# Attention kernel's first 25 microseconds: first weights moved to ScalarE's queue behind its statistics, block 0 of x loaded in four pieces on two queues, first half of K turned ahead of the norms

## The chip, the cores and the metric

The kernel runs on one core of a Trainium2 chip. The metric is the device time of one execution in microseconds (us), median and mean over several runs, always compared with runs of the kernel before from the same rounds on the same chip. A profile is one traced execution of the same program; its span leaves out about 1.8 us that the device time includes (1939.6 against 1941.37 us in the profiled run of the kernel before).

Engine names: PE is TensorE (matmuls and transposes), PEld its weight loads, DVE is VectorE, ACT is ScalarE, POOL is GpSimd, SP is SyncE. A "q" (ACTq, SPq) marks an engine's sequencer issuing a DMA.

## The reference, cut to what matters

```python
def reference(A_x, A_k_cache, A_v_cache, A_wq, A_wo, B_x, B_w1, B_w3, B_w2):
    xn = layernorm(A_x)                     # 2048 x 640
    q  = (xn @ A_wq) in 32 heads of 192
    o  = softmax(q @ k_cache^T * 192**-0.5) @ v_cache     # per head, 2048 keys
    s  = o @ A_wo
    g  = silu((silu(xn @ B_w1) * (xn @ B_w3)) @ B_w2)     # hidden size 1536
    return A_x + s * g
```

The attention of 32 heads is nearly all of the work. Before its first score can be computed, the first block of x (512 rows) must be loaded, normalised, turned (transposed) and projected with the weights of head 0, and the first half of K must be loaded and turned.

## The kernel before: what the change touches

`load_x(g, t0, t1, queue)` loads tiles t0 to t1 of x's block g. `ln_stats`, `ln_rstd` and `ln_norm` are the norm on VectorE, with the reciprocal root on GpSimd; `ln_stats_act` does tile 3's statistics on ScalarE. `ln_turn` transposes two tiles on TensorE and copies the result to `xnT`; `kn` is K as loaded, `pk0` and `pk1` hold its turned halves in PSUM, `KW` holds them in SBUF; `swap_halves` makes a copy of xnT with its halves of the partitions exchanged, by DMA (`xnS`).

```python
    def load_w0():
        W = wqp.tile([P, 2 * DC, P], BF16, tag="W", name="W")
        nc.gpsimd.dma_start(out=W[:, 0:DC, :], in_=A_wq[:, 0:P]...)       # runs of 256 bytes
        nc.gpsimd.dma_start(out=W[:, DC:2 * DC, 0:PGW], in_=gate_cols(0)...)  # runs of 128 bytes
        nc.gpsimd.dma_start(out=W[:, DC:2 * DC, PGW:P], in_=A_wq[:, P:DH]...)
        ...
    def copy_k0(copy, src, half, two):          # a copy of turned K out of PSUM
        KW = loads[0]["KW"]
        ks = slice(half * HP * P, (half + 1) * HP * P)
        copy(out=KW[:, 0:2, ks] if two == 0 else KW[:, 2:5:2, ks], in_=src[:, 2 * two:2 * two + 2, :])
    ...
    pk1 = ps_o.tile([P, 4, 512], BF16, tag="ob1", name="pk1")    # two banks of PSUM
    warm = pk1[:, 0, 0:2 * P].bitcast(F32)

    def turn_over(k):                           # k dummy matmuls
        for i in range(k):
            nc.tensor.matmul(warm, lhsT=ident_bf[:], rhs=ident_bf[:], start=True, stop=True)

    def head_start():
        load_x(0, 0, 2)
        load_x(0, 2, 4)
        load_k0(0, nc.sync)                     # K of head 0, first half
        load_w0()
        turn_over(34)
        ln_stats(0, 0)
        ln_stats(0, 1)
        ln_stats_act(0, 3)
        load_k0(1, nc.scalar)
        load_x(1, queue=nc.scalar)
        load_v(0, (0,), nc.scalar)
        ln_stats(0, 2)
        ...                                     # two small VectorE instructions
        ln_rstd(0, 3)
        load_w(1)
        for i in range(4):
            ln_norm(0, i, nc.vector)
        pk0 = ps_o.tile([P, 4, 512], BF16, tag="ob0", name="pk0")
        turn_k0(pk0, 0, range(4))               # 16 transposes of K
        copy_k0(nc.scalar.copy, pk0, 0, 0)
        turn_over(4)
        ln_turn(0, 0, nc.scalar.copy)
        turn_k0(pk1, 1, (0, 1))                 # 8 transposes of K's second half
        ln_turn(0, 1, nc.vector.tensor_copy)
        swap_halves(0)
        copy_k0(nc.scalar.copy, pk0, 0, 1)
        copy_k0(nc.vector.tensor_copy, pk1, 1, 0)
        load_v(0, (1,))
        load_x(2)
        project_first()                         # the first projection
        turn_k0(pk1, 1, (2, 3))                 # the other 8
        copy_k0(nc.scalar.copy, pk1, 1, 1)
        scores(0)
        shift_first()                           # VectorE: two shifts of q
        shift_k0()                              # VectorE: "K shift", KW<-KW
        scores(1)
        ln_stats(1, 0)                          # the norms of block 1 follow
        ...
```

## Time and profile before

| | before |
|---|---|
| device time, first three runs | 1940.66, 1940.94, 1941.77 us |
| span of the profile | 1939.6 us |
| PE busy | 99% |
| PE share of the chain that ended last | 98% |
| PE time lost between matmuls after 62 us, as recorded | 1.3 us |

"Lost" in the last row is the sum of all stretches over 40 ns by which a matmul starts later than the columns of the matmul before it need at full clock. It is counted from the starts in the TensorE timeline. Most of it is not real: this profile has eight matmul records fewer than weight loads (see the counts below), and four of the eight stretches, of 0.22 to 0.23 us, are about as long as one matmul of 512 columns at full clock.

The first section and the chain section of the page of the kernel before (engine, busy us, share of the span):

```profile
PE 1928.9 (99%) x27267; PEld 1317.8 (68%) x27275; DVE 654.2 (34%) x997; ACT 1181.2 (61%) x1278; POOL 282.6 (15%) x501
...
PE 98%; DVE 1%; DMA 0%; ACT 0%; issue 0%; SPq 0%; POOL 0%; DVEq 0%; ACTq 0%
```

So the whole question is at what time TensorE gets into its steady rhythm. The TensorE timeline of the kernel before (start in us, duration, engine, line, operation, tiles, shape, count, and in brackets the idle time before and what ended it):

```profile
2.77 3.81 PE L569 MATMUL pk<-ident_bf 128*128 128x128 bf16 x34 [2.77 <-POOL ident_bf masks.py:199]
7.90 1.07 PE L271 MATMUL pk<-ident_bf,kn 128*128 128x128 bf16 x16 [1.32 <-DMA kn<-in_A_k_cache_dram]
...
9.03 0.72 PE L354 MATMUL pst<-ident_bf,xn 128*128 128x128 bf16 x10
...
11.20 2.34 PE L391 MATMUL ps<-xnT,W 128*128 128x256 bf16 x20 [0.44 <-ACT xnT L356]
```

and, from the timeline of its weight loads, the load that opens the turn of block 1's last tiles (the turn itself starts at 23.86):

```profile
23.85 0.56 PEld L354 LDWEIGHTS <-xn 128*128 128x128 bf16 x10 [0.36 <-DVE qA L429]
```

34 dummy matmuls keep TensorE busy while x and K arrive; TensorE pauses 1.32 us for K; x is turned at 9.03; the projection starts at 11.20. At 23.86 TensorE waits for VectorE's cast of qA. The VectorE timeline shows why:

```profile
11.53 0.68 DVE L277 COPY KW<-pk 128x1024 bf16<-128x1024 bf16 x1
...
13.58 0.42 DVE L393 CAST qA<-ps 128x256 bf16<-128x256 f32 x1 [0.67 <-PE ps L391]
...
14.88 0.42 DVE L281 COPY KW<-KW 64x1024 bf16<-64x1024 bf16 x1
15.33 0.89 DVE L316 BATCH_NORM_STATS2 stats<-x_all 128x6 f32<-128x320 bf16 x2
...
22.12 0.88 DVE L316 BATCH_NORM_STATS2 stats<-x_all 128x6 f32<-128x320 bf16 x2
23.04 0.21 DVE L317 BATCH_NORM_AGGREGATE mv<-stats 128x2 f32<-128x12 f32 x1
23.16 0.64 DVE L429 CAST qA<-ps 128x512 bf16<-128x512 f32 x1
```

From the first projection's casts on, VectorE works through copies, shifts and the norms of block 1 and the first of block 2 almost without a gap (one of 0.81 us, for GpSimd's reciprocal root), and the cast that TensorE needs stands in order behind all of it. From 15 to 24 us VectorE sets the pace. K's copy on VectorE at 11.53 falls into a lull before the casts.

### The profile page before, as it was taken

To read this page: it belongs to the slowest core of one execution; us is meant where nothing else is said; L and a number is where in the kernel's file an instruction comes from. 1 tells how busy PE (TensorE), PEld (TensorE's weight loads), DVE (VectorE), ACT (ScalarE), POOL (GpSimd) and SP (SyncE) were. 2 spreads that over 40 slices of the span, in tenths; PEclk is the share of its full clock that TensorE was granted. 3 is DMA by queue.
4 is the path that set the end of the run, shared out by engine and by line. 5 is a ranking of instruction groups with operands and counts; after the bars stand their busy time and mean duration, and the time that the engine had idled before them with its cause. 6 is when DMAs were issued, how large, how long until landed. Compare 5 with 4: busy or idle time off the path is not lost.

```text
span 1939.6 us, 59659 instructions
## 1 busy us (share of the span) xinstructions
PE 1928.9 (99%) x27267; PEld 1317.8 (68%) x27275; DVE 654.2 (34%) x997; ACT 1181.2 (61%) x1278; POOL 282.6 (15%) x501
## 2 busy tenths in 40 slices
PE   8999999999999999999999999999999999999998
PEld 6666666666666666666666666666666666577776
DVE  7333333333333333333333333333333334521111
ACT  6667676767776767776777777677767677210000
POOL 3111111111111111111111111111111110000000
PEclk9999999999999999999999999999999999999999
DMA  8643433323233434363434343434333220937882
GB/s 178 132 101 64 101 68 83 86 56 91 58 89 65 98 63 99 68 162 68 101 64 101 68 101 68 100 66 100 69 68 90 63 70 2 259 70 135 152 152 61
DMA packets 394643, 178.98 MB, mean 92 GB/s; under 512 B 341616, under 2 KB 382832, under 8 KB 394384
## 3 DMA queue, kind: packets, MB, share of 16 engines
q1 hardware_dynamic: 371136, 125.32, 30.9%
q0 software_dynamic: 19472, 45.71, 9.8%
q8 instruction: 215, 3.52, 0.8%
q10 hardware_dynamic: 3776, 4.06, 0.7%
q14 instruction: 44, 0.36, 0.1%
HBM read 52.82 MB, written 27.79 MB: 42 GB/s over the span
## 4 chain that ended last, share of the span: by engine, by line
PE 98%; DVE 1%; DMA 0%; ACT 0%; issue 0%; SPq 0%; POOL 0%; DVEq 0%; ACTq 0%
PE obank L516 35%; PE st L487 33%; PE ps L424 14%; PE ps_s L111 11%; PE ps_f L728 3%; PE ps_gu L702 1%; PE st L488 1%; PE ps L410 0%; DMA kn<-in_A_k_cache_dram 0%; DVE stats L316 0%; PE ps L391 0%; DVE xn L346 0%; DVE mv L317 0%; DVE qA L429 0%; ACT xnT L356 0%
## 5 line engine op out<-in xcount | busy, mean ns | idle before, releaser
L490 ACT ACTIVATE pT<-st 128x1024 bf16<-128x1024 f32 x1024 | 1047.1, 1023 | 251.1 <-PE st L488 235.6
L516 PEld LDWEIGHTS <-pT 64*128 64x128 bf16 x16384 | 713.7, 94 | 242.2 <-ACT pT L490 0.2
L516 PE MATMUL obank<-vt,pT 64*128 64x193 bf16 x16384 | 851.8, 243 | 0.0
L487 PE MATMUL st<-qC,KW 64*128 64x512 bf16 x2046 | 605.6, 376 | 0.1
L525 DVE COPY osum<-obank 128x772 f32<-128x772 f32 x128 | 123.1, 962 | 788.8 <-PE obank L516 788.8
L488 PE MATMUL st<-qB,KW 64*128 64x512 bf16 x1024 | 385.0, 376 | 0.0
L487 PE MATMUL st<-qA,KW 64*128 64x512 bf16 x1022 | 384.3, 376 | 0.4 <-ACT pT L490 0.3
L488 PE MATMUL st<-qC,KW 64*128 64x512 bf16 x1022 | 384.3, 376 | 0.0
L488 PE MATMUL st<-qA,KW 64*128 64x512 bf16 x1022 | 384.3, 376 | 0.0
L487 PEld LDWEIGHTS <-KW 64*128 64x128 bf16 x3068 | 278.0, 94 | 153.8 <-issue 2.1
L424 PE MATMUL ps<-xnT,W 64*128 64x512 bf16 x1280 | 297.2, 376 | 0.0
L424 PE MATMUL ps<-xnS,W 64*128 64x512 bf16 x1280 | 296.3, 376 | 0.0
L488 PEld LDWEIGHTS <-KW 64*128 64x128 bf16 x3068 | 278.0, 94 | 0.7 <-issue 0.6
L377 POOL DMA_DIRECT2D qC<-qA x124 | 65.4, 528 | 1285.6 <-DVE rl_all L532 1270.0
L430 ACT CAST qB<-ps 128x512 bf16<-128x512 f32 x131 | 76.8, 586 | 228.3 <-PE ps L424 222.7
L111 PE MATMUL ps_s<-wo_sb,oT 128*128 128x384 bf16 (+3 forms) x1535 | 208.8, 299 | 0.1
L424 PEld LDWEIGHTS <-W 64*128 64x128 bf16 x2560 | 122.9, 94 | 121.2
L111 PEld LDWEIGHTS <-oT 128*128 128x128 bf16 x1536 | 148.4, 98 | 60.4
L526 DVE TENSOR_TENSOR osum<-osum,obank 128x772 f32<-128x772 f32 x128 | 122.7, 958 | 13.4
L533 DVE TENSOR_TENSOR ostage<-osum,rl_all 128x768 bf16<-128x768 f32 x128 | 122.7, 958 | 4.4
L465 DVE SCALAR_TENSOR_TENSOR hT<-pt,qB 64x512 bf16<-64x512 bf16 x64 | 43.8, 684 | 199.4 <-ACT pt L464 199.4
L429 DVE CAST qA<-ps 128x512 bf16<-128x512 f32 x131 | 90.5, 691 | 25.2 <-PE ps L410 7.2
(84 smaller groups left out, 622.4 us busy)
## 6 DMA issues: line engine op xcount, KB each, us to landing
o_scr<-ostage SPq DMA_DIRECT2D x16, 1536.0 KB, 10.3
vt<-in_A_v_cache_dram SPq DMA_DIRECT2D x63, 384.0 KB, 5.7
qC<-qA POOLq DMA_DIRECT2D x248, 64.0 KB, 1.9
qC<-qB POOLq DMA_DIRECT2D x124, 64.0 KB, 2.4
wo_sb<-in_A_wo_dram POOLq DMA_DIRECT2D x1, 7680.0 KB, 36.2
W<-in_A_wq_dram POOLq DMA_DIRECT2D x32, 160.0 KB, 3.4
W<-in_B_w_dram POOLq DMA_DIRECT2D x32, 80.0 KB, 3.2
W<-in_A_wq_dram POOLq DMA_DIRECT2D x32, 80.0 KB, 2.9
```

Source lines behind the costliest of these rows:

```text
L111: nc.tensor.matmul(ps[:, 0:w], lhsT=oT[:, k, :], rhs=wo_sb[:, k, c0:c1], start=(k == 0), stop=(k == OC - 1))
L377: nc.gpsimd.dma_start(out=qC[0:64, half, :], in_=qAB[half][64:P, :])
L424: nc.tensor.matmul(ps[:, r * 512:(r + 1) * 512], lhsT=W[rows, j, :], rhs=xs[rows, j // 2, qs], start=(j == 0), stop=(j == 2 * DC - 1))
L429: a = nc.vector.tensor_copy(out=qAB[0][:], in_=ps[:, 0:512])
L430: b = nc.scalar.copy(out=qAB[1][:], in_=ps[:, 512:1024])
L487: nc.tensor.matmul(st2[:, 0:512], lhsT=ka, rhs=qa, start=r == 0 and nr == 3, stop=r == nr - 1)
L488: nc.tensor.matmul(st2[:, 512:1024], lhsT=kb, rhs=qb2, start=r == 0 and nr == 3, stop=r == nr - 1)
L490: nc.scalar.activation(out=pT2[:], in_=st2[:], func=ACT.Exp, scale=att_scale)
L516: nc.tensor.matmul(obanks[r][:, j * 256:j * 256 + DH + 1], lhsT=pT2[r * 64:(r + 1) * 64, t * 512 + j * P:t * 512 + (j + 1) * P], rhs=vt[r ...
L525: nc.vector.tensor_copy(out=osum[:], in_=ov[0])
L526: nc.vector.tensor_tensor(out=osum[:], in0=osum[:], in1=ov[1], op=ALU.add)
L533: nc.vector.tensor_tensor(out=ostage[:, qb * 4:qb * 4 + 4, hg * DH:(hg + 1) * DH], in0=osum[:, :, 0:DH], in1=rl.unsqueeze(2).to_broadcast( ...
```

## The change

Intent: get x and K in first, so that the first projection starts sooner, by keeping head 0's weights out of the first microseconds; and let ScalarE copy the turned x before it copies K. The diff, cut to its core:

```diff
-    def load_w0():
+    def load_w0(queue):
...     (nc.gpsimd.dma_start becomes queue.dma_start, three times)
@@ loads_after, in the middle of the kernel
-            for c0, c1 in _pieces(FC, -(-FC // 6)):
+            for c0, c1 in _pieces(FC, -(-FC // 2)):
@@ head_start
-        load_x(0, 0, 2)
-        load_x(0, 2, 4)
+        for t in range(4):
+            load_x(0, t, t + 1, nc.scalar if t % 2 else nc.sync)
         load_k0(0, nc.sync)
-        load_w0()
-        turn_over(34)
+        turn_over(24)
         ln_stats(0, 0)
         ln_stats(0, 1)
         ln_stats_act(0, 3)
+        load_w0(nc.scalar)
         load_k0(1, nc.scalar)
         load_x(1, queue=nc.scalar)
-        load_v(0, (0,), nc.scalar)
...
+        load_v(0, (0,), nc.gpsimd)
         load_w(1)
...
         turn_k0(pk0, 0, range(4))
-        copy_k0(nc.scalar.copy, pk0, 0, 0)
+        turn_over(12)
+        ln_turn(0, 0, nc.scalar.copy)
         turn_over(4)
-        ln_turn(0, 0, nc.scalar.copy)
-        turn_k0(pk1, 1, (0, 1))
         ln_turn(0, 1, nc.vector.tensor_copy)
         swap_halves(0)
+        copy_k0(nc.scalar.copy, pk0, 0, 0)
         copy_k0(nc.scalar.copy, pk0, 0, 1)
-        copy_k0(nc.vector.tensor_copy, pk1, 1, 0)
         load_v(0, (1,))
         load_x(2)
         project_first()
-        turn_k0(pk1, 1, (2, 3))
-        copy_k0(nc.scalar.copy, pk1, 1, 1)
+        turn_k0(pk1, 1, range(4))
+        copy_k0(nc.scalar.copy, pk1, 1, 0)
+        copy_k0(nc.vector.tensor_copy, pk1, 1, 1)
         scores(0)
```

The change also loads w2, used near the end, in two pieces instead of six.

More of the change, by code (lines that the diff above doesn't have):

```diff
@@ L219, in gate_cols @@
         return wsel[:, (h // 2) * PGW:(h // 2 + 1) * PGW]
-    def load_w0():
+    def load_w0(queue):
         W = wqp.tile([P, 2 * DC, P], BF16, tag="W", name="W")
-        nc.gpsimd.dma_start(out=W[:, 0:DC, :], in_=A_wq[:, 0:P].rearrange("(c p) d -> p c d", p=P))
-        nc.gpsimd.dma_start(out=W[:, DC:2 * DC, 0:PGW], in_=gate_cols(0).rearrange("(c p) f -> p c f", p=P))
-        nc.gpsimd.dma_start(out=W[:, DC:2 * DC, PGW:P], in_=A_wq[:, P:DH].rearrange("(c p) d -> p c d", p=P))
+        queue.dma_start(out=W[:, 0:DC, :], in_=A_wq[:, 0:P].rearrange("(c p) d -> p c d", p=P))
+        queue.dma_start(out=W[:, DC:2 * DC, 0:PGW], in_=gate_cols(0).rearrange("(c p) f -> p c f", p=P))
+        queue.dma_start(out=W[:, DC:2 * DC, PGW:P], in_=A_wq[:, P:DH].rearrange("(c p) d -> p c d", p=P))
         loads.setdefault(0, {}).update(W=W)
```

## The prediction

> **What bounds the kernel now.** The page puts PE busy at 99% of 1939.6 us and the chain that ended last at 98% PE. From the PE timeline, stretches where matmuls start further apart than their columns need add up to under 0.7 us after 60 us. Only the first 36 us can give anything back: 0.1% or so.
>
> **The start, before** (timelines by engine). x lands at 3.59 and 4.35 us; VectorE's statistics start at 3.62, norms 0 and 1 end at 7.93. K's first half, behind x, lands at 7.85, so PE idles 1.3 us (waits), turns K from 7.90, and first turns x at 9.03. ScalarE copies K (9.00) before xnT (9.91 to 11.14); the projection starts at 11.20. Its VectorE casts end at 14.00, three 0.29 us shifts and a 0.42 us K shift at 15.30; first exp at 15.05. VectorE then works almost unbroken to 23.80, where its cast of qA holds PE (0.29 us).
>
> **What the change does.**
> - Four x loads on two queues: the same bytes. The gain is the smaller first load, an estimated 0.4 us for VectorE's start; the Trainium skill, "DMA: Bandwidth & Descriptors", section "Issuing engines are not separate DMA queues", says more issuers save only issue time.
> - W of head 0 leaves the first microseconds: the identity may be ready at 1.7 instead of 2.7 us (GpSimd spends 1.02 us on a W load inside it), K's first half lands near 5.2. W, issued near 5.0-6.5 on ScalarE, should land by 9 (now 8.28).
> - K is turned before the norms end, so x's first turn follows norm 1 (7.6) and ScalarE copies xnT first: projection near 9.6, 1.6 us earlier.
> - But the second K half moves behind the projection: 16 transposes there instead of 8, and VectorE's 0.68 us copy, formerly in a lull at 11.53, now stands before the shifts. First exp near 13.7; K shift ends near 14.7, only 0.6 earlier.
> - Dummies 24+12+4 against 34+4 fill waits. The skill, "TensorE: Matmul & The Clock Gate", Part 1, says about 3.4 us of activity releases the clock; this trace agrees (107 ns steps until about 6.3 us, 56 later). The pause before K could delay that by some tenths.
> - w2 in two loads: issued at 844 us, first used at 1673. Nothing.
>
> **How much is critical.** PE and ScalarE get some 1.4 us ahead at the first scores, but from 15 to 24 us VectorE's chain sets the pace, and it gains what the projection gains less about 0.95. I expect the 0.29 us stall near 23.9 to grow to about 1 us and swallow the rest. Net gain about 0.5 us.
>
> **Prediction.** 1940.4 us, 8 in 10 between 1939.4 and 1941.3. Faster by over 2%: 0.003; within 2%: 0.994; slower: 0.003.
>
> **What would show each step.** Timeline: first statistics near 3.2; K landing near 5.2; first xnT copy from 8.3; projection near 9.6; first exp near 13.7; K shift ending near 14.7; PE stall before the turn near 23 about 1 us; VectorE statistics in the chain of waits from 15 to 24. After 40 us the two timelines keep a constant offset: the gain.
>
> **What would make it wrong.** W landing after 9.6 (small pieces) would hold the projection and could leave no gain. V's first half, now on GpSimd's queue behind the roots, landing after 15.4 would hold the values. A cold PE clock at the projection costs up to 1 us. If VectorE is not the limit before 24 us, up to 1.4 us is gained.

## The result, and the profile after

| | before | after |
|---|---|---|
| device time, median of six runs | 1942.16 us (1940.66 to 1942.61) | 1943.49 us (1943.04 to 1944.24) |
| mean of the six | 1941.86 us | 1943.51 us |
| span of the profile | 1939.6 us | 1941.6 us |

The ratio is 1.0009, 95% interval 0.9996 to 1.0021. Ratios here are the mean time of one kernel's runs over the mean of the other's of the same rounds, so not quite the ratio of the medians. All six runs of the changed kernel are slower than all six of the kernel before, and the profiles differ by 2.0 us: it is slightly slower, where a gain of 0.5 us had been predicted.

The TensorE timeline of the changed kernel:

```profile
1.38 2.74 PE L569 MATMUL pk<-ident_bf 128*128 128x128 bf16 x24 [1.38 <-POOL ident_bf masks.py:199]
6.09 1.89 PE L271 MATMUL pk<-ident_bf,kn 128*128 128x128 bf16 x16 [1.98 <-DMA kn<-in_A_k_cache_dram]
7.78 1.34 PE L569 MATMUL pk<-ident_bf 128*128 128x128 bf16 x12
8.96 0.72 PE L354 MATMUL pst<-ident_bf,xn 128*128 128x128 bf16 x10
...
10.99 2.34 PE L391 MATMUL ps<-xnT,W 128*128 128x256 bf16 x20 [0.53 <-ACT xnT L356]
...
21.36 0.39 PE L424 MATMUL ps<-xnS,W 64*128 64x512 bf16 x2 [0.21 <-DMA xnS<-xnT]
...
23.30 0.38 PE L424 MATMUL ps<-xnT,W 64*128 64x512 bf16 x1
...
25.84 0.73 PE L354 MATMUL pst<-ident_bf,xn 128*128 128x128 bf16 x10 [0.85 <-DVE qA L429]
```

Read it against the one before. K is there at 6.09 instead of 7.90. But the same 16 transposes take 1.89 us instead of 1.07: the clock of TensorE is not up yet (its matmuls of 128 columns start 107 ns apart, where later it is 56), and the 12 dummies after them are slow too, so x is turned at 8.96, hardly earlier than 9.03, although its norm was ready at 8.19. The projection gains 0.21 us, not 1.6. And at the end of the stretch the same turn that stood at 23.86 stands at 25.84, almost 2 us later.

The VectorE timeline of the changed kernel:

```profile
13.37 0.42 DVE L393 CAST qA<-ps 128x256 bf16<-128x256 f32 x1 [0.67 <-PE ps L391]
13.83 0.29 DVE L396 COPY qC<-qB 64x512 bf16<-64x512 bf16 x1
15.31 0.69 DVE L277 COPY KW<-pk 128x1024 bf16<-128x1024 bf16 x1 [1.19 <-ACT KW L277]
...
16.56 0.42 DVE L281 COPY KW<-KW 64x1024 bf16<-64x1024 bf16 x1
...
24.10 0.89 DVE L316 BATCH_NORM_STATS2 stats<-x_all 128x6 f32<-128x320 bf16 x2 [0.22 <-DMA x_all<-in_A_x_dram]
...
25.15 0.64 DVE L429 CAST qA<-ps 128x512 bf16<-128x512 f32 x1
```

VectorE's K copy waits 1.19 us for ScalarE's K copy, and the K shift ends at 16.98 instead of 15.30. The statistics of block 2 then wait for x of block 2, which landed at 24.08 (before: 21.82, without a wait). The losses account for the whole 1.99 us at this point:

- projection: -0.21 us
- projection to the end of the K shift: +1.89 us (5.99 against 4.10), of which 1.19 is the wait and 0.7 the copy itself, which before had run in the lull
- x of block 2: +0.31 us (from the norm at 23.08 to the statistics 1.02 us, against 0.71 before)

This is a sum along VectorE's way. The loads are a second late path beside it: VectorE was ready at 23.88, only 0.2 us before x landed, so mending one of the two alone gives back little.

Why is x of block 2 late? These are the traffic windows before the projection (window, length, then busy us of each engine, clock, share of the DMA engines' time, GB/s), first of the kernel before:

```profile
5.00:6.00 1.00, 1.00 (x12) 1.00 (x11) 0.93 (x5) 0.97 (x4) 0.00 (x0) 1.00 0.84 273
6.00:7.00 1.00, 0.58 (x6) 0.31 (x3) 0.94 (x3) 0.16 (x2) 0.72 (x1) 1.00 0.85 203
7.00:8.00 1.00, 0.10 (x2) 0.10 (x3) 0.93 (x4) 0.00 (x0) 0.69 (x1) 1.00 1.01 324
```

and of the changed kernel:

```profile
5.00:6.00 1.00, 0.00 (x0) 0.00 (x0) 0.96 (x4) 0.97 (x3) 0.00 (x0) 1.00 0.17 65
6.00:7.00 1.00, 0.91 (x9) 0.91 (x10) 0.95 (x3) 0.51 (x2) 0.71 (x1) 1.00 0.20 46
7.00:8.00 1.00, 1.00 (x13) 1.00 (x11) 0.95 (x5) 0.00 (x0) 0.45 (x2) 1.00 0.90 177
```

The DMA engines stand idle for most of two microseconds: x and K are in, and the next loads, starting with W, only go out when ScalarE's queue has passed its statistics, which wait for x. Everything behind is shifted: x of block 1 lands at 12.69 (before 10.85), the swapped halves of xnT at 19.74 and 21.32 (before 16.92 and 19.00), x of block 2 at 24.08 (before 21.82). The chain of waits of the changed kernel shows the end of this, an x load that it did not contain before:

```profile
13.03 1.25 SPq L289
...
14.32 9.76 DMA x_all<-in_A_x_dram
...
24.10 0.90 DVE stats L316 x2
...
25.23 0.56 DVE qA L429
```

After that the two profiles run in parallel: TensorE loses the same after 62 us in both, at the same places.

A caution for readers of such pages: in these windows "PEclk" (the column before the DMA share) reads 1.00 from the start, while the dummies step by 107 ns, nearly twice the 56 ns of later. The record of the clock in the trace begins only when the clock first changes; before it, the durations must be read. I use that first record below: it is at 6.73 us in the kernel before and at 8.84 us in the changed one.

### The profile page after: what moved, and what is told of

It reads as the page before. It is cut to its first block, busy times and chain, and to the rows that moved or that the text cites. A ratio compares the mean times of both kernels' runs of the same rounds, so it can differ in the third digit from the quotient of the medians.

```text
span 1941.6 us, 59662 instructions
## 1 busy us (share of the span) xinstructions
PE 1930.2 (99%) x27269; PEld 1318.6 (68%) x27277; DVE 654.5 (34%) x997; ACT 1181.1 (61%) x1278; POOL 281.0 (14%) x499
## 4 chain that ended last, share of the span: by engine, by line
PE 98%; DMA 1%; DVE 0%; ACT 0%; SPq 0%; issue 0%; DVEq 0%; ACTq 0%
PE obank L516 35%; PE st L487 33%; PE ps L424 14%; PE ps_s L111 11%; PE ps_f L728 3%; PE ps_gu L702 1%; PE st L488 1%; DMA x_all<-in_A_x_dram 1%; PE ps L410 0%; DMA kn<-in_A_k_cache_dram 0%; PE pk L271 0%; DVE stats L316 0%; PE pst L354 0%; SPq L289 0%; ACT xnT L356 0%
## 6 DMA issues: line engine op xcount, KB each, us to landing
o_scr<-ostage SPq DMA_DIRECT2D x16, 1536.0 KB, 10.3
```

## The experiments

Three candidates came out of the comparison: the **wait** between the two K copies, the **DMA** hole through W's new place, and the **clock**. The rival to all three was that the new order of work itself is worse. Each edit below is against the changed kernel unless said otherwise. Every run gave a correct result. The mean differences below are to the mean of nine runs of the kernel before from the same rounds; they have an uncertainty of some tenths of a us that I estimate from the scatter of single runs. The intervals are wider, about ±0.0014 (2.7 us), and contain 1 in all but two cases (e4_warm, e6_w0gp), so times are compared only where the two sets of five runs, of the same rounds, stay apart or nearly so.

### First call: the wait and the DMA hole, alone and together

The control, the changed kernel unedited:

> The changed kernel itself, as a control in the same rounds as the next three. Both theories: 1 to 2 us slower than the kernel before (ratio about 1.0005 to 1.001), with K's second copy on VectorE starting near 15.3 us, its K shift ending near 17.0, x of block 2 landing near 24.1, and a PE stall of 1.0 us near 25.8.

`e1_nodep`: the two copies read one tile, pk1, but different banks of it. The Trainium skill, "PSUM — Partial Sum Buffer", section "Terms", gives a bank as 2 KiB per partition and says that two engines on the same bank at once are an error, reads included. Each half of pk1 is 2 x 512 x 2 bytes, exactly a bank, and the copies take one half each, so the order between them can go (it is per tile where the hardware's rule is per bank); no run raised an error or gave a wrong result.

```diff
-        copy_k0(nc.scalar.copy, pk1, 1, 0)
-        copy_k0(nc.vector.tensor_copy, pk1, 1, 1)
+        c0 = copy_k0(nc.scalar.copy, pk1, 1, 0)       # copy_k0 now returns the instruction
+        c1 = copy_k0(nc.vector.tensor_copy, pk1, 1, 1)
+        tc.declare_no_dep(c1.ins, c0.ins, reason="two banks, two destinations")
```

> The changed kernel with the order between the two copies out of one PSUM tile released (two banks, two destinations). Wait theory: VectorE's copy starts near 14.3 instead of 15.31 and its K shift ends near 16.0 instead of 16.98; if that wait alone is the cause, the kernel comes back by about 1 us. DMA theory: x of block 2 still lands near 24.1, so VectorE waits there 1.1 us longer instead, the PE stall near 25.8 keeps its size, and the gain is under 0.2 us.

`e2_w0sync`: W goes on the sync queue directly behind K's first half.

```diff
         load_k0(0, nc.sync)
+        load_w0(nc.sync)
...
-        load_w0(nc.scalar)
```

> The changed kernel with W of head 0 issued on the sync queue right behind K's first half instead of on ScalarE's queue behind its statistics. DMA theory: the hole in the DMA traffic from 5 to 7.5 us closes, K's second half and x of block 1 land about 1.5 us earlier, x of block 2 near 22.5; if DMA alone is the cause, the kernel comes back by over 1 us. Wait theory: VectorE's copy still waits for ScalarE's, K shift still ends near 17.0, and only about 0.3 us comes back.

`e3_nodep_w0sync`: both edits.

> Both together. If the two are parallel late paths into the same VectorE statistics, each alone gives 0.3 us or less and both give about 1 us or more: K shift ending near 16.0, x of block 2 near 22.5, VectorE's cast of qA near 24.2 instead of 25.15. If their effects simply add, this run gives the sum of the two single ones.

Measured (positions in us in each run's one profile; "clock" is the first record of the clock in its trace):

| run | mean minus before | profile | clock | projection | K shift ends, after projection | xnS lands | x of block 2 lands |
|---|---|---|---|---|---|---|---|
| before | | 1939.6 | 6.73 | 11.20 | 4.10 | 19.00 | 21.82 |
| after | +1.7 | 1941.6 | 8.84 | 10.99 | 5.99 | 21.32 | 24.08 |
| e0_after | +1.5 | 1940.8 | 4.40 | 10.07 | 5.99 | 20.48 | 23.34 |
| e1_nodep | +1.4 | 1940.9 | 10.34 | 11.54 | 4.95 | 20.45 | 23.24 |
| e2_w0sync | +2.1 | 1942.3 | 10.80 | 12.04 | 5.98 | 19.15 | 21.81 |
| e3_nodep_w0sync | +0.9 | 1941.6 | 10.66 | 12.15 | 4.95 | 19.19 | 21.89 |

Two of the candidates are shown in these positions. Releasing the copies takes 1.04 us off the way from the projection to the K shift, in both runs that have it and in none that lacks it. This is the VectorE line in e1:

```profile
14.82 0.69 DVE L277 COPY KW<-pk 128x1024 bf16<-128x1024 bf16 x1
```

the bracket with the 1.19 us is gone. And W behind K brings the two late landings back to where they were before the change, in both runs that have it. In the window from 5 to 6 us, e2 moves 267 GB/s where the changed kernel moved 65.

The absolute expectations failed, and so did the simple sum: I expected K shifts ending at 16.0 and got 16.49 (e1) and 17.10 (e3), because the clock came late in these profiles and moved the projection. The control, whose clock came early, had its positions 0.7 to 0.9 us ahead of what I expected (K shift 16.06, x of block 2 23.34). Alone, neither edit won time: e1 equals the control, e2 is 0.6 us slower. With W behind K in both, the release is worth 1.2 us (e2 against e3: 1943.49 to 1944.34 against 1942.27 to 1943.37, no overlap). With W late it is worth nothing measurable. With the copies released in both, moving W is worth 0.5 us (e1 against e3), but these two sets overlap. That W's place costs time thus rests more on the landings than on the times. Why e2 is slower than the control is not shown; with W behind K, K lands 0.4 us later (6.45 against 6.03), which lengthens TensorE's pause before it. In e1 the statistics of block 2 start at 23.31, as x lands (23.24): the two late paths end within 0.1 us of each other there, although the clock differs too, so this one run does not separate them cleanly.

The control against the first profile of the same kernel shows the third candidate at once. The TensorE timeline of e0_after, the same program as after:

```profile
6.08 1.07 PE L271 MATMUL pk<-ident_bf,kn 128*128 128x128 bf16 x16 [1.96 <-DMA kn<-in_A_k_cache_dram]
...
10.07 2.34 PE L391 MATMUL ps<-xnT,W 128*128 128x256 bf16 x20
```

The 16 transposes take 1.07 us here and 1.89 there, and the projection starts 0.92 us earlier. The Trainium skill, "TensorE: Matmul & The Clock Gate", Part 1, section "What's actually happening", says that the clock is released after a busy window of about 3.4 us and that these windows run freely, whatever the kernel does. The traces agree that the moment is luck from one execution to the next: with 24 dummies, then a pause of 1.9 to 2.6 us for K, the first record of the clock was at 4.4, 8.8, 10.3, 10.7 and 10.8 us. The first two are the same program.

### Second call: the pause filled, and a version meant to beat both

`e4_warm`: 48 dummies, so that TensorE does not pause before K.

```diff
-        turn_over(24)
+        turn_over(48)
```

> The changed kernel with 48 dummy matmuls in place of 24 ahead of K, so that TensorE has no pause before K's first half lands. Clock theory: in the four traces of the changed kernel and its variants so far, the matmul step falls from 107 to 56 ns at 4.4, 8.8, 10.3 and later, whichever window the pause falls into; without the pause it falls before 8 us, the projection starts at 10.2 or earlier, and the best and the worst of five runs lie closer together. Against the run of e0_after whose clock came at 4.4 us there is no gain; against the profile of after (8.8 us) about 0.9 us on the projection. Wait and DMA theories alone: no change in time, since the VectorE copy still waits for ScalarE's and x of block 2 lands after 23 us.

`e5_nodep_w0sync_warm`: the edits of e1, e2 and e4.

> Released copies, W behind K's first half on the sync queue, and 48 dummies. If clock, copies and W's place are the whole of the loss: projection near 10.3, K shift ending near 15.3 (as before), x of block 2 near 22, PE stall near 24 about 0.3 to 0.5 us, time equal to the kernel before within 0.5 us, so 1 to 1.5 us faster than the changed one. If some other part of the change costs, it stays above the kernel before by 1 us.

`e10_mix`: W behind K and 48 dummies; from the kernel before, x in two loads, V's first half on ScalarE's queue, and half of K's second half turned and copied ahead of the projection.

```diff
-        for t in range(4):
-            load_x(0, t, t + 1, nc.scalar if t % 2 else nc.sync)
+        load_x(0, 0, 2)
+        load_x(0, 2, 4)
         load_k0(0, nc.sync)
-        turn_over(24)
+        load_w0(nc.sync)
+        turn_over(48)
...
-        load_w0(nc.scalar)
...
         load_x(1, queue=nc.scalar)
+        load_v(0, (0,), nc.scalar)
...
-        load_v(0, (0,), nc.gpsimd)
...
-        turn_over(12)
+        turn_over(4)
...
         swap_halves(0)
+        turn_k0(pk1, 1, (0, 1))
         copy_k0(nc.scalar.copy, pk0, 0, 0)
         copy_k0(nc.scalar.copy, pk0, 0, 1)
+        copy_k0(nc.vector.tensor_copy, pk1, 1, 0)
...
-        turn_k0(pk1, 1, range(4))
-        copy_k0(nc.scalar.copy, pk1, 1, 0)
-        copy_k0(nc.vector.tensor_copy, pk1, 1, 1)
+        turn_k0(pk1, 1, (2, 3))
+        copy_k0(nc.scalar.copy, pk1, 1, 1)
```

> A version meant to beat both: x in two loads, W behind K's first half on the sync queue, 48 dummies, K's first half turned ahead of the norms with ScalarE copying xnT first as in the change, but half of K's second half turned and copied by VectorE before the projection as in the kernel before, and V's first half on ScalarE's queue again. If the account is right: statistics from 3.6, projection near 10.2 (1.0 earlier than before), K shift ending near 14.3, x of block 2 near 21, profile 0.5 to 1.0 us shorter than the kernel before's. If VectorE's chain is not what decides, no gain.

`e11_before_warm`: the kernel before with `turn_over(54)` in place of `turn_over(34)`.

> The kernel before with 54 dummies in place of 34, so that TensorE works until K lands at 7.85. Clock theory: the kernel before has the same exposure (1.3 us pause, then K), so some of its runs start the turns cold; with the pause filled its slower runs go, and the spread of its times shrinks, the fastest staying where they are or 0.3 us slower. If the kernel before is not exposed, nothing changes or it is up to 0.7 us slower.

| run | five runs, us | mean minus before | profile | clock | projection | K shift ends | xnS lands | x of block 2 lands |
|---|---|---|---|---|---|---|---|---|
| e4_warm | 1943.88 to 1945.72 | +3.1 | 1943.3 | 5.39 | 10.03 | 16.02 | 22.26 | 25.02 |
| e5_nodep_w0sync_warm | 1941.31 to 1942.08 | +0.2 | 1940.1 | 5.82 | 10.04 | 14.99 | 19.58 | 22.47 |
| e10_mix | 1940.98 to 1941.54 | -0.3 | 1939.6 | 7.17 | 10.13 | 14.24 | 19.13 | 22.00 |
| e11_before_warm | 1940.99 to 1942.07 | +0.1 | 1940.0 | 7.84 | 11.48 | 15.59 | 19.20 | 21.96 |

The clock did what was expected: 48 dummies bring it before 8 us in every profile. But e4 is the slowest kernel of the call, which no theory had foreseen. Its TensorE timeline:

```profile
19.82 0.38 PE L424 MATMUL ps<-xnT,W 64*128 64x512 bf16 x1
22.30 0.50 PE L424 MATMUL ps<-xnS,W 64*128 64x512 bf16 x2 [2.11 <-DMA xnS<-xnT]
...
25.92 0.38 PE L424 MATMUL ps<-xnT,W 64*128 64x512 bf16 x1
```

and two of its windows (the columns as above; the clock is the third number from the end):

```profile
22.00:23.00 1.00, 0.70 (x5) 0.32 (x6) 0.80 (x2) 0.00 (x0) 0.07 (x1) 0.73 3.21 82
23.00:24.00 1.00, 1.00 (x8) 0.52 (x6) 0.00 (x0) 0.00 (x0) 0.00 (x0) 0.50 0.06 26
```

TensorE arrives a microsecond earlier at the projection of head 1, whose swapped halves of xnT are late (22.26), and waits 2.1 us. Right after it the clock is halved again, from 22.46 to 25.88 in the trace's record. That costs about 1.7 us: from the first to the last start of this group 3.62 us pass here (22.30 to 25.92), 1.94 in the changed kernel. So in this profile the early clock bought a longer wait, and the wait cost clock. The DMA hole alone does not do it: e0_after has the hole and the projection as early (10.07), but there the halves landed at 20.48 and the wait was 0.29 us. Why the loads were later still in e4 is not shown; the two ran on different chips.

With W behind K (e5) the halves land at 19.58, nothing of the kind happens, and the kernel is within 0.24 us of the kernel before, and within 0.14 us of the kernel before with its own pause filled (e11): clock, copies and W's place together make up nearly all of the loss. The rival, that the order of work itself costs a microsecond, falls. The order is not free, though: the way from the projection to the end of the K shift is still 4.95 us in e5, against 4.10 before, which the earlier projection (10.04 against 11.20) pays for. And TensorE's stall at its turn, expected at 0.3 to 0.5 us, was 1.1; VectorE waited 0.60 us for x of block 2 there.

e10 reached its K shift (14.24, expected 14.3) but not its gain: VectorE was ready a microsecond early and then waited for x of block 2, which lands at 22.00 as ever. e11 suggests that the kernel before is exposed too: its nine runs of this call lie in two groups, six from 1940.76 to 1941.22 and three from 1942.55 to 1943.30, while the five with the pause filled lie from 1940.99 to 1942.07. That the upper group is the late clock is likely but not traced in those runs (e8, below, traces such a start). Filling the pause did not lower the mean (+0.1).

### Third call: the clock in one pair, the x load, and W's move undone

`e13_nodep_w0sync_again` is the kernel of e3, `e14_nodep_w0sync_warm_again` that of e5, this time in the same rounds.

> The same kernel as e3_nodep_w0sync (24 dummies), repeated as the partner of the next run in the same rounds. Clock theory: wherever the record of the released clock comes after 8 us in its profile, the projection starts after 11 us; its times lie 0.5 to 1.5 us above those of the next run. Rival: the difference of e3 and e5 came from the chip and the rounds alone; then the two agree within 0.3 us.

> The same kernel as e5_nodep_w0sync_warm (48 dummies), repeated in the same rounds as its partner with 24. Clock theory: full clock before 8.3 us, projection near 10.0, spread of the five times under 1 us, and 0.5 to 1.5 us faster than the partner.

e13 took 1942.16 to 1943.32 us (mean +1.3), e14 1941.28 to 1942.19 (mean +0.3). The only difference is 24 dummies. The TensorE timeline of e13:

```profile
6.74 1.89 PE L271 MATMUL pk<-ident_bf,kn 128*128 128x128 bf16 x16 [2.62 <-DMA kn<-in_A_k_cache_dram]
...
12.20 1.03 PE L391 MATMUL ps<-xnT,W 128*128 128x256 bf16 x8 [0.53 <-ACT xnT L356]
```

and of e14:

```profile
6.29 1.07 PE L271 MATMUL pk<-ident_bf,kn 128*128 128x128 bf16 x16 [0.83 <-DMA kn<-in_A_k_cache_dram]
...
10.04 2.35 PE L391 MATMUL ps<-xnT,W 128*128 128x256 bf16 x20
```

The first record of the clock is at 10.67 and at 4.01 us, the projection 2.16 us apart, the means 1.0 us apart. With the other two causes removed, the clock is worth 1 us; the two sets of times touch by 0.03 us. The rival (chip and rounds), which expected the two to agree within 0.3 us, falls.

`e12_mix_x2early`: e10 with x of block 2 issued before V's second half.

```diff
-        load_v(0, (1,))
         load_x(2)
+        load_v(0, (1,))
```

> The mixed version with x of block 2 issued ahead of V's second half on the sync queue. In the mixed version VectorE was ready for its statistics of block 2 about 1 us before x of block 2 landed (22.0), which held the cast of qA and stalled TensorE 1.12 us at 23.77. DMA theory: x of block 2 lands near 20.5, the cast comes near 22.1, the stall falls to about 0.3 us, the profile is near 1938.7, and the time 0.7 to 1.2 us below the kernel before. If V's second half now lands too late for the values near 23, TensorE waits there instead and nothing is gained.

It took 1940.19 to 1940.95 us, mean 0.9 us below the kernel before of the same rounds (1940.67 to 1942.46); ratio 0.9996, interval 0.9982 to 1.0009; profile 1938.5. x of block 2 landed at 20.56. The VectorE timeline of e12, to be read against 22.12 and 23.16 before:

```profile
20.89 0.88 DVE L316 BATCH_NORM_STATS2 stats<-x_all 128x6 f32<-128x320 bf16 x2
21.81 0.21 DVE L317 BATCH_NORM_AGGREGATE mv<-stats 128x2 f32<-128x12 f32 x1
21.93 0.64 DVE L429 CAST qA<-ps 128x512 bf16<-128x512 f32 x1
```

and its weight load for the turn, to be read against 23.85 and its wait of 0.36 before:

```profile
22.73 0.56 PEld L354 LDWEIGHTS <-xn 128*128 128x128 bf16 x10 [0.16 <-DVE qA L429]
```

The 1.12 us of lead over the kernel before at this point is the 1.1 us by which the profile is shorter. This is the fastest version. Its interval does not exclude "no difference" from the kernel before, and two of the nine runs of the kernel before lie among its five; the trace shows where the microsecond between these two profiles comes from.

`e6_w0gp`: only W's move undone.

```diff
         load_k0(0, nc.sync)
+        load_w0(nc.gpsimd)
...
-        load_w0(nc.scalar)
```

> The changed kernel with only W's move undone: head 0's W is back on GpSimd's queue in the first microseconds. If W's move is what made the later transfers late, x of block 2 lands near 22 and the moved half of xnT near 19.2 (after: 24.1 and 21.3), while K's first half lands near 7.5 and the identity is ready near 2.7 as before. The copies still wait for each other, so the K shift ends no earlier than 16.0 and it stays 0.5 to 1.5 us slower than the kernel before. If the order of the work alone is at fault, x of block 2 stays after 23 us.

The later transfers came back as expected: x of block 2 at 22.37, the swapped halves at 19.58. But K landed at 5.81 us, not near 7.5, and the runs without a profile were far slower than the profiled one: 1942.65 (profiled) against 1944.19 to 1945.32. The five are 3.1 us above the kernel before, where 0.5 to 1.5 had been expected. That raised two questions.

### Fourth call: what was still open

`e15_w0gp_warm`: e6 with `turn_over(40)`.

> The changed kernel with W back on GpSimd (as e6_w0gp) and 40 dummies in place of 24. In e6 the four runs without a profile were 1.5 to 2.7 us longer than the profiled one, whose clock came at 8.4 us. Clock theory: those had it later, because 24 dummies from 2.8 us on leave a pause; with 40 the clock comes by 8 us and the times fall by 1 to 2 us to about 1942.5 with a spread under 1.5 us. Rival, another cost of W on GpSimd: the times stay near 1944.5 though the clock comes early.

`e16_before_x2early`: the kernel before with the edit of e12 alone.

> The kernel before with only x of block 2 issued ahead of V's second half. In the kernel before VectorE reached its statistics of block 2 at 22.12, x of block 2 had landed at 21.82: it was not waiting. So no gain (within 0.3 us), though x lands near 20.4; the gain of e12 then needs the earlier projection and the shorter VectorE chain too. If it is 0.6 us or more faster, e12 owes its gain to this line alone.

`e17_before_x4`: the kernel before with the four x loads alone.

> The kernel before with only the four x loads on two queues. e6 had K's first half at 5.81 with W on GpSimd in place, so I expect the four loads, not W's move, to bring K forward: landing below 6.3 instead of 7.4 to 7.9, while the first statistics stay at 3.7 to 3.9. The turns of K then end before the norms, the projection comes 0.3 to 0.9 us earlier if the clock is up in time, and the time is equal to the kernel before or up to 0.5 us lower. If K still lands after 7, W's move brought it forward after all.

`e8_before_w2`: the kernel before with w2 in two loads alone.

> The kernel before with only w2 in two loads instead of six. Issued near 844 us, first used at 1673: no difference beyond the spread of the kernel before (mean within 0.4 us).

| run | five runs, us | mean minus before | clock | first statistics | K lands | projection |
|---|---|---|---|---|---|---|
| e6_w0gp | 1942.65 to 1945.32 | +3.1 | 8.37 | 3.95 | 5.81 | 10.65 |
| e15_w0gp_warm | 1942.25 to 1943.55 | +1.7 | 5.83 | 4.08 | 7.88 | 11.54 |
| e16_before_x2early | 1940.89 to 1942.62 | +0.2 | 5.52 | 3.81 | 7.44 | 10.79 |
| e17_before_x4 | 1941.03 to 1942.37 | +0.1 | 5.93 | 3.82 | 7.54 | 10.88 |
| e8_before_w2 | 1941.66 to 1942.65 | +0.8 | 11.60 | 3.89 | 7.37 | 12.11 |

- e15 fits the clock theory in its fall of 1.3 us and its narrower spread; it came to 1943.1 where I expected 1942.5. Its profile still has the wait between the copies and a K shift ending at 17.52.
- e16 gains nothing, as expected: the x load order is worth something only when VectorE gets there earlier. e12's gain does not come from this line alone. e10, which lacks only this line, was 0.3 us below the kernel before; the other parts were not tested one by one.
- e17 contradicts my reading of e6. With W on GpSimd's queue, K landed at 7.37 to 7.88 in every profile but e6's (seven with it: before, e6, e8, e11, e15, e16, e17); with W behind ScalarE's statistics at 5.91 to 6.05, behind K on the sync queue at 6.25 to 6.69. W's move did bring K forward. Why e6 had it at 5.81 stays open.
- e17 also shows that four loads on two queues do not start the norm earlier: first statistics at 3.82, like 3.81 and 3.89 of two that load x in two pieces.
- e8 missed its expectation by a little in time (+0.8 against 0.4). Its profile has the clock at 11.60, the latest of all, and TensorE loses the same as in the kernel before after 62 us, at the same places, none of them near 844. I take the difference for the clock, but one profile doesn't show what its other runs had. Its TensorE timeline is what an unlucky run of the kernel before looks like:

```profile
7.41 1.89 PE L271 MATMUL pk<-ident_bf,kn 128*128 128x128 bf16 x16 [0.83 <-DMA kn<-in_A_k_cache_dram]
...
12.11 1.14 PE L391 MATMUL ps<-xnT,W 128*128 128x256 bf16 x9
```

## Why the prediction was wrong, point by point

The prediction was wrong in its direction: 0.5 us of gain forecast, about 1.7 us of loss measured (mean of six against six). Its sum along VectorE's way was 1.6 gained at the projection less 0.95, so 0.65 us; the profile has 0.21 less 1.89 less 0.31, so -1.99. Of the 2.64 us between them, 1.39 is the projection (point 2), 0.94 the way to the K shift (point 1) and 0.31 x of block 2 (point 4).

1. **"It gains what the projection gains less about 0.95."** This step failed in every profile of the changed kernel, whatever the clock. The form is right: VectorE's chain did set the pace, up to its last wait for x, and TensorE did stall 1.0 us at its turn (25.84). The 0.95 was mis-sized: the way from the projection to the end of the K shift grew by 1.89 us. I had counted the extra copy (0.68) but not that it waits for ScalarE's copy from the same tile (1.19). The kernel's code releases just such a pair of casts elsewhere, with the reason "two banks, two destinations"; that should have made me ask it of the new pair. e1, e3 and e5 show it: the way shrinks by 1.04 us when the order is released; the other 0.15 us of the wait is not due to the order.
2. **"Projection near 9.6, 1.6 us earlier."** It came at 10.99, or 10.07 in the profile with an early clock. I had listed the clock as "some tenths" and under "what would make it wrong" as up to 1 us. It is 0.92 us between two profiles of the same program, and 1.0 us in time between e13 and e14. The cause is the cut from 34 to 24 dummies together with an identity that is ready earlier: the dummies end at 4.1 us and K comes at 6.1. The prediction took the kernel before as agreeing with a release after about 3.4 us of activity. Its trace is weak evidence for that: all 34 dummies step by 107 ns, the record of the release is 3.96 us after the first of them, and in the nine profiles whose matmuls ran unbroken until the release (e4, e5, e10, e11, e12, e14 to e17) it came 2.6 to 5.8 us after the first.
3. **"The gain is the smaller first load, an estimated 0.4 us."** There is none. The first statistics started at 3.87 (before 3.62), and in e17 and its neighbours they start together. All four tiles share the same engines; here the Trainium skill's sentence that I quoted beside the estimate ("DMA: Bandwidth & Descriptors", "Issuing engines are not separate DMA queues") should have been believed against it.
4. **"W ... should land by 9."** It landed at 10.14, still in time for the projection. What I did not ask is what stands behind W: two idle microseconds of the DMA engines, and every later load pushed back, up to x of block 2 by 2.26 us. In the profile of the changed kernel this adds only 0.31 us, because VectorE was late as well; it becomes the limit when VectorE is earlier (e1: statistics at 23.31, x at 23.24). e2, e3 and e5 show that W's place is the cause of the late landings.
5. Right: nothing is to be had after 40 us; w2's loads move nothing that a trace shows; the identity is ready earlier (1.38 us); K lands earlier through W's move (6.05; predicted 5.2); V's first half on GpSimd's queue landed at 14.87, ahead of its first use at 17.48.

What stays open: why K landed at 5.81 us in e6 alone; why the loads from V's first half on landed 1.7 to 2.3 us later in e4 than in e0_after, which issued them at nearly the same times (x of block 2 at 13.78 there, 14.10 in e4); why e2 was slower than the control; and the clock in runs without a profile, which can only be guessed from their times.

## What to carry to other kernels

A wait that is removed pays only if the next one behind it is gone too: here two late paths ended 0.2 us apart and a late clock moved both. Each of the three edits alone gained nothing or lost, and together they undid the loss (e5). Only a further rearrangement came out below the kernel before (e12, by about 0.9 us in the mean, which its interval does not secure). When a load is moved out of the way, look at what the DMA engines do in the time it leaves free and which loads stand behind it in its new queue; and when copies are regrouped, ask of each pair on two engines whether it now reads one tile. Dummy matmuls for the clock must reach to the first real work without a pause, because a few microseconds of start-up can otherwise differ by one microsecond from run to run and hide every smaller effect.

## What the Trainium skill lacked or had wrong

- "TensorE: Matmul & The Clock Gate", Part 1, "What you observe" gives the transition at about 4 us of sustained activity, ±500 ns from run to run. Where the activity has a pause the spread is much larger: two profiles of one program had it at 4.4 and 8.8 us, and variants with the same 24 dummies at 10.3 to 10.8. With no pause it came 2.6 us (e14) to 5.8 us (e10) after the first matmul. The page doesn't say that dummies which end before the real work can miss the window altogether.
- The same page, "HAM oscillation — how this bites in real kernels", puts the rule at idle gaps of over about 3.4 us. In e4_warm a gap of 2.1 us was followed by half the clock for 3.4 us (22.46 to 25.88), worth about 1.7 us (3.62 us against 1.94 for the same group of matmuls). The clock fell 17.07 us after its release, five times the 3.41 us that the slow stretch lasted, which fits a gap judged inside a window of that length; one trace shows it.
- "PSUM — Partial Sum Buffer" gives the rule for two engines by bank. No page says that two copies by two engines out of different banks of one tile are put in order by the tile unless released; VectorE's copy waited 1.19 us here, and releasing the order took 1.04 us off its way.
- "DMA: Bandwidth & Descriptors" says that several issuers save only issue time, and the runs agree (first statistics at 3.82 with four loads on two queues, 3.81 and 3.89 with two on one). It doesn't spell out that a queue whose engine waits for data holds back all the loads behind it: 65 and 46 GB/s in two windows of 1 us where there had been 273 and 203.
